# A decode kernel of two layers: the mixer's two halves of w3 in two PSUM banks, and a new order at the start of layer 2

## The chip, the cores and the metric

The kernel runs on one core of one Trainium2 chip. The metric is the time of one execution in microseconds (us), taken on the device. Before the change it was 529.77 us (median of 6 runs, 528.97 to 530.6). Every run also has a *span*, the time from the core's first to its last profiled instruction.

## The reference

One token (a row of 640) passes attention, mixer, attention, mixer; both layers use the same weights and caches.

```python
def _A_ref(x, k_cache, v_cache, wq, wo):          # 32 heads of 192
    W = 4096                                       # the last 4096 of 32768 positions
    q = (x @ wq) ...                               # one query for each head
    scores = einsum(q, k_cache[:, :, Sk - W:]) * 192 ** -0.5
    o = einsum(softmax(scores), v_cache[:, :, Sk - W:])
    return o @ wo
def _B_ref(x, w1, w2, w3, w4):
    ...                                            # with one token, the shifted part adds nothing
    h2 = gelu(layernorm(x1) @ w3) @ w4             # 640 -> 1536 -> 640
    return x1 + h2
x = x + _A_ref(layernorm(x), ...)                  # layer 1
x = x + _B_ref(layernorm(x), ...)
x = x + _A_ref(layernorm(x), ...)                  # layer 2, the same caches
x = x + _B_ref(layernorm(x), ...)
```

K and V of a head are 4096 x 192 bf16, 1536 KB each. Loading them is nearly all of the work.

## The kernel before

SBUF holds eleven *cells* of 1536 KB: one holds K or V of a head, transposed K, a block of wo, w3 or w4. A load is issued by the Sync engine's queue (SPq) in a fixed order, and each waits until its cell has been given back.

Layer 1 ends with heads 0 to 3, and layer 2 starts with them, to use again what is still on chip. K of heads 0 to 6 stays, transposed, in seven cells (the *kept* heads). V 3 stays in its cell. A part of V 2 stays in PSUM: while layer 1 uses V 2, VectorE turns (transposes) 22 units of 96 words per partition into four banks of PSUM and, for what doesn't fit there, into the free end of the bank in which O is accumulated. At the start of layer 2 it turns them back into SBUF. Only the rest of V 2 is loaded again.

In the views PE is TensorE, PEld its loading of weights, DVE VectorE and ACT ScalarE. *PV* is the product of a head's softmax weights (`PT`) with its V, which TensorE accumulates in the bank of O. K 8 is K of head 8, V 2 is V of head 2.

```python
VC, VP, VW = 3, 2, 22 * Dh // 2        # kept V, parked V, parked words per partition
...
O_bank = psO.tile([P, 512], F32, name="O_ps")      # one bank
O_ps = O_bank[:, 0:2 * Dh]
VB = 2048
V_bank = psV.tile([P, VB], F32, name="V_ps")       # four banks
VX = 2 * Dh, 2 * Dh + VW - VB

def v_words(layer):                    # layer 0: SBUF -> PSUM; layer 1: PSUM -> SBUF
    V = need("v", layer, VP)
    step = 512
    for i in range(0, VW, step):
        n = min(step, VW - i)
        a = V[:, 2 * i:2 * (i + n)].bitcast(U32)
        b = (V_bank[:, i:i + n] if i < VB else O_bank[:, VX[0]:VX[1]]).bitcast(U32)
        nc.vector.transpose(b if layer == 0 else a, a if layer == 0 else b)
```

(In the code layers are 0 and 1; the text says layer 1 and layer 2.) The first step of attention in layer 2, with the next heads 4 to 7 of which 4, 5 and 6 are kept:

```python
# after the scores of heads 0..3
q1[0]()            # PE: the projection of heads 4..7, 30 matmuls
q1[1]()
part_max()         # DVE: softmax of heads 0..3 begins
q1[2]()
turn_max()
q1[3]()
full_max()
for i, (q2, h2) in enumerate(keep):          # scores of heads 4, 5, 6
    for half in range(2):
        T(h2, half)
        S(h2, half, ST_n, q2)
    if i == 0:
        spread_max()
turn_p()
need("v", 1, cur[-1] + 1)
q[0]()
PT = swap()
...
q[2]()
v_words(1)         # the turn of V 2, just ahead of the first PV
q[3]()
```

The mixer's first product, in both layers. One column of `hp` holds 128 of the 1536 outputs and takes five matmuls:

```python
for half in range(2):
    hp = O_bank[:, VX[1] + half * HF:VX[1] + (half + 1) * HF]    # both in the bank of O
    for i in range(HF):                                          # HF = 6
        for kc in range(ND):                                     # ND = 5
            nc.tensor.matmul(hp[:, i:i + 1], lhsT=w3[kc][:, ...], rhs=xc[:, kc:kc + 1], ...)
    h_ps.append(hp)
for half, hp in enumerate(h_ps):
    nc.scalar.activation(sq[:], hp, ACTF.Square, scale=rr[:, 0:1])
    ...                                                          # the rest of gelu, then hT
# then 60 matmuls of w4, of which the first 30 need half 0 alone
```

Of the kernel before, what the change touches and what calls it, by code (L numbers as in the profile page):

```python
# [9 lines left out]
F32 = mybir.dt.float32  # L10
U32 = mybir.dt.uint32
# [6 lines left out]
P = 128  # L18
# [8 lines left out]
def kernel(  # L27
# [16 lines left out]
    _, H, Sk, Dh = A_k_cache.shape  # L44
# [6 lines left out]
    ND, NF = D // P, F // P  # L51
# [12 lines left out]
    NA = Dh // 32  # L64
    NKEEP, NCELL = 7, 11
    WARM = 29
    VC, VP, VW = 3, 2, 22 * Dh // 2
    W3C, W4C = FREE // F, FREE // D
    assert W4C % 2 == 1 and W4C < NF
    GROUPS = [[list(range(h, h + QH)) for h in range(0, H, QH)] for _ in range(2)]  # L70
# [9 lines left out]
    psV = ctx.enter_context(tc.tile_pool(name="psV", bufs=1, space=PSUM))  # L80
# [4 lines left out]
        name=nc.get_next_instruction_name(), act_func_set_id=ACT_TABLE_SET, ins=[], outs=[]))  # L85
# [381 lines left out]
    O_bank = psO.tile([P, 512], F32, name="O_ps")  # L467
    nc.vector.memset(O_bank[:], 0.0)
    O_ps = O_bank[:, 0:2 * Dh]
    VB = 2048  # L470
    V_bank = psV.tile([P, VB], F32, name="V_ps")
    VX = 2 * Dh, 2 * Dh + VW - VB

    def v_words(layer):
        V = need("v", layer, VP)
        step = 512
        for i in range(0, VW, step):
            n = min(step, VW - i)
            a = V[:, 2 * i:2 * (i + n)].bitcast(U32)
            b = (V_bank[:, i:i + n] if i < VB else O_bank[:, VX[0]:VX[1]]).bitcast(U32)  # L480
            nc.vector.transpose(b if layer == 0 else a, a if layer == 0 else b)

    def pv(layer, h, hq, PT, mid=None):
# [41 lines left out]
    def attention(layer, x_cur, rs_cur, x_new, z_new, rs_new, ss_new):  # L525
# [8 lines left out]
        def softmax_scale():  # L534
            rstd = power(total()[:, 0:1], 1.0 / D, eps1[:], "rstd")
            nc.vector.tensor_scalar(out=sc[:], in0=rstd[:], scalar1=scale, scalar2=None, op0=ALU.mult)
# [51 lines left out]
        q1 = qproj_steps(groups[1][0] // QH, xc)  # L588
        for hq, h in enumerate(groups[0]):
            for half in range(2):  # L590
                if layer == 0:
                    T(h, half)
                else:
                    Th.update({(h, q): transpose_quart(layer, h, q) for q in (2 * half, 2 * half + 1)})
                S(h, half, ST, hq)
                if (hq, half) == (0, layer):
                    qb[2]()
                    qb[3]()
            if hq == 1:
                softmax_scale()  # L600
        pending = None
        early = None
        for gi, cur in enumerate(groups):
            nxt = list(enumerate(groups[gi + 1])) if gi + 1 < len(groups) else []
            ST_n = None
            if nxt:
                part_max, turn_max, full_max, spread_max, turn_p, swap, recip = softmax_steps(len(cur), ST, sc)
                ST_n = next_scores()
                if layer == 1 and gi == 0:
                    keep = [hh for hh in nxt if hh[1] < NKEEP]  # L610
                    del nxt[:len(keep)]
                    q = qproj_steps(groups[2][0] // QH, xc)
                    q1[0]()
                    q1[1]()
                    part_max()
                    q1[2]()
                    turn_max()
                    q1[3]()
                    full_max()
                    for i, (q2, h2) in enumerate(keep):  # L620
                        for half in range(2):
                            T(h2, half)
                            S(h2, half, ST_n, q2)
                        if i == 0:
                            spread_max()
                    turn_p()
                    need("v", 1, cur[-1] + 1)
                    q[0]()
                    PT = swap()
                    q[1]()  # L630
                    rl = recip()
                    q[2]()
                    v_words(1)
                    q[3]()
                else:
                    if gi == 0:
                        for step in q1:
                            step()
                    h0 = nxt[0][1]
                    T(h0, 0)  # L640
                    part_max()
                    T(h0, 1)
                    S(h0, 0, ST_n, 0)
                    turn_max()
                    full_max()
                    S(h0, 1, ST_n, 0)
                    spread_max()
                    h1 = nxt[1][1]
                    q = None
                    if gi + 2 < len(groups):  # L650
                        q = qproj_steps(groups[gi + 2][0] // QH, xc)
                    if q:
                        q[0]()
                    if pending is not None:
                        y_ps = out_proj(layer, *pending)
                    turn_p()
                    T(h1, 0)
                    if q:
                        q[1]()
                        q[2]()  # L660
                    if pending is not None:
                        add_y(y_ps, 2)
                        pending = None
                    PT = swap()
                    T(h1, 1)
                    if q:
                        q[3]()
                    rl = recip()
                    nxt.pop(0)
            else:  # L670
                PT, rl = early
            oT = sm.tile([P, NA], BF16, name="oT")
            hurry = gi + 2 == len(groups)
            final = gi + 1 == len(groups)
            fold = None
            order = list(enumerate(cur))
            if layer == 1 and gi == 0:
                order.insert(0, order.pop(cur.index(VC)))
            for hq, h in order:
                o_sb = pv(layer, h, hq, PT, fold)  # L680
                if final:
                    if layer == 0 and hq == 0:
                        add_y(out_proj(layer, *pending), 1)
                    if layer == 0 and hq == 1:
                        center_y()
                    fold = None
                    if hq < QH - 2:
                        o_fold(h, o_sb, oT, rl)
                    else:
                        def fold(h=h, o_sb=o_sb):  # L690
                            o_fold(h, o_sb, oT, rl)

                    continue
                if hurry and hq == 1:
                    (q2, h2), (q3, h3) = nxt
# [3 lines that stand above are left out]
                    T(h3, 0)  # L699
                    S(h3, 0, ST_n, q3)  # L700
                    T(h3, 1)
                elif hurry and hq == 2:
                    S(h3, 1, ST_n, q3)
                    steps = softmax_steps(len(cur), ST_n, sc)
                    steps[0]()
                    steps[1]()
                elif nxt and not (hurry and hq == 3):
                    q2, h2 = nxt.pop(0)
# [3 lines that stand above are left out]
                o_fold(h, o_sb, oT, rl)  # L712
                if hurry and hq == 2:
                    steps[2]()
                if hurry and hq == 3:
                    for step in steps[3:5]:
                        step()
                    early = steps[5](), steps[6]()
            if final:
                if layer == 1:  # L720
                    y_ps = out_proj(layer, *pending)
                    fold()
                    add_y(y_ps, 1)
                    center_y()
                else:
                    fold()
            pending = (cur[0] // QH, oT)
            ST = ST_n
        add_y(out_proj(layer, *pending), 0)

    def mixer(layer, x_cur, z, rs_cur, ss_cur, x_new, rs_new):
# [23 lines left out]

        HF = NF // 2
        hT = big.tile([P, NF], BF16, name="hT")
        h_ps = []
        for half in range(2):
            hp = O_bank[:, VX[1] + half * HF:VX[1] + (half + 1) * HF]  # L760
            for i in range(HF):
                fc = half * HF + i
                f0 = 2 * P * (fc // 2) + fc % 2
                for kc in range(ND):
                    nc.tensor.matmul(
                        hp[:, i:i + 1], lhsT=w3[kc][:, f0:f0 + 2 * P - 1:2], rhs=xc[:, kc:kc + 1],
                        start=(kc == 0), stop=(kc == ND - 1))
            h_ps.append(hp)
        for half, hp in enumerate(h_ps):
            sq = sm.tile([P, HF], F32, name="sq")  # L770
            nc.scalar.activation(sq[:], hp, ACTF.Square, scale=rr[:, 0:1])
# [75 lines left out]
```

## Time and profile before

| what | before | where to read it |
|---|---|---|
| time | 529.77 us, 6 runs | times |
| moved by DMA | 217.31 MB, 98.0% of 16 engines' span | page |
| rate, 20 to 285 us and 305 to 500 us | 423 to 430 GB/s | windows |
| rate, 285 to 305 us (between the layers) | 345 GB/s | windows |
| busy: PE, DVE | 60%, 54% | page |
| last wo landed, then serial work to the end | 516.85 us, about 12 us (to the end of the span, 528.6 us) | chain of waits |

These are lines of the page of the kernel before: the span, TensorE's busy time, what the DMA engines moved, the main queue, and the share of each engine in the chain of waits that ended last.

```profile
span 528.6 us, 10089 instructions
PE 318.6 (60%) x4421; PEld 194.2 (37%) x4421; DVE 285.1 (54%) x557; ACT 41.0 (8%) x157; POOL 2.7 (1%) x12
...
DMA packets 23823, 217.31 MB, mean 411 GB/s; under 512 B 2532, under 2 KB 3044, under 8 KB 8292
...
q1 hardware_dynamic: 23780, 216.67, 98.0%
...
DMA 47%; PE 27%; DVE 20%; issue 4%; ACT 1%; SPq 1%; DVEq 0%; ACTq 0%
```

The next view gives the windows of the kernel before. The columns are the stretch, its length, busy time of each engine with the number of instructions, and at the end the granted clock, the DMA engines' busy share and GB/s.

```profile
20.00:285.00 265.00, 160.06 (x2042) 94.82 (x2043) 150.08 (x257) 17.37 (x66) 0.00 (x0) 0.67 1.01 423
285.00:305.00 20.00, 16.00 (x401) 12.85 (x399) 5.92 (x38) 3.78 (x17) 0.00 (x0) 0.68 0.90 345
305.00:320.00 15.00, 8.62 (x125) 4.64 (x121) 8.30 (x17) 0.78 (x3) 0.00 (x0) 0.66 1.02 430
```

The DMA engines are full (a share of 1.01 or 1.02) before and after the stretch between the layers, and not in it. A chain of waits with PE and DVE in it does not contradict this: each load waits for a cell, but while several loads are queued nothing is lost by that wait. Time can only be won where the DMA engines run dry, from 285 to 305 us, and in the tail, after the last load that anything waits for.

The timeline of the kernel before, in the first mixer. Columns: start, duration, engine, line, operation, out<-in, number, and in brackets the idle time ahead and what ended it.

```profile
286.93 0.24 PE L765 MATMUL O_ps<-xc,cell_2816 128*128 128x1 bf16 x4
...
288.50 0.17 PE L765 MATMUL O_ps<-xc,wx_sb 128*128 128x1 bf16 x1
...
288.76 0.27 ACT L771 ACTIVATE sq<-O_ps,r 128x6 f32<-128x6 f32 x1 [0.85 <-PE O_ps L765]
...
289.46 0.25 ACT L771 ACTIVATE sq<-O_ps,r 128x6 f32<-128x6 f32 x1
...
290.13 1.11 PE L792 MATMUL y_ps<-hT,cell_2995 128*128 128x1 bf16 x33 [1.47 <-DVE gu L773]
```

The 60 matmuls of w3 run from 286.93 to 288.67 us. The first Square reads only half 0, which was complete after 30 of them, but it starts at 288.76, after all 60, released by PE.

The same view at the start of layer 2: the turn of V 2 in five pieces (4 + 1), and the first PV matmuls.

```profile
306.66 2.49 DVE L481 STREAM_TRANSPOSE cell_3350<-V_ps 128x512 uint32<-128x512 uint32 x4
309.07 0.21 DVE L481 STREAM_TRANSPOSE cell_3350<-O_ps 128x64 uint32<-128x64 uint32 x1
...
309.33 1.45 PE L492 MATMUL O_ps<-cell_2819,PT 128*2 128x384 bf16 x16 [2.72 <-DVE cell_3350 L481]
```

And the Sync queue's timeline: when loads went out.

```profile
285.82 0.33 SPq L127 DMA_DIRECT2D cell_3344<-in_A_v_cache_dram  x1
291.92 0.33 SPq L127 DMA_DIRECT2D cell_3346<-in_A_v_cache_dram  x1
295.85 0.33 SPq L109 DMA_DIRECT2D cell_3348<-in_A_k_cache_dram  x1
...
299.45 0.33 SPq L109 DMA_DIRECT2D cell_3354<-in_A_k_cache_dram  x1
```

The load at 291.92 goes into the cell that w4 leaves at the end of the first mixer; the one at 295.85 into the cell of the first kept head, after its scores.

### The profile page before, as it was taken

The numbers are of one execution on the slowest core, as the hardware profiler recorded it, in microseconds if no ns is written. First come the engines' busy times: TensorE is split into PE (matmuls) and PEld (weight loads), VectorE is DVE, ScalarE is ACT, GpSimd is POOL, SyncE is SP. The second block draws the span as 40 slices with busy tenths as digits, with TensorE's granted clock in tenths as the row PEclk, the third lists the DMA queues.
The fourth block names the chain that finished last, engine by engine and source line by source line (L and its number), as shares of the span: only waits on it lengthen the run. The fifth ranks groups of instructions, "written<-read, shape, count | busy, mean of one in ns | idle before, by whom it ended". The sixth has DMA issues, their size and how long they took to land.

```text
span 528.6 us, 10089 instructions
## 1 busy us (share of the span) xinstructions
PE 318.6 (60%) x4421; PEld 194.2 (37%) x4421; DVE 285.1 (54%) x557; ACT 41.0 (8%) x157; POOL 2.7 (1%) x12
## 2 busy tenths in 40 slices
PE   1057657666563755746654865666666655647755
PEld 1023434343341533424323633434343433424325
DVE  2067655576464665556632255666665664646623
ACT  1000101010100001001101101010010001001011
POOL 2000000000000000000000000000000000000000
PEclk9999975557666576557655767675567676557655
DMA  8999999999999999999999899999999999999993
GB/s 346 430 423 425 423 427 425 422 426 421 427 424 421 425 424 426 423 425 423 424 408 391 326 428 428 421 425 421 428 422 427 424 424 425 423 425 422 425 411 127
DMA packets 23823, 217.31 MB, mean 411 GB/s; under 512 B 2532, under 2 KB 3044, under 8 KB 8292
## 3 DMA queue, kind: packets, MB, share of 16 engines
q1 hardware_dynamic: 23780, 216.67, 98.0%
q8 instruction: 34, 0.56, 0.4%
q14 instruction: 9, 0.07, 0.0%
HBM read 216.66 MB, written 0.00 MB: 410 GB/s over the span
## 4 chain that ended last, share of the span: by engine, by line
DMA 47%; PE 27%; DVE 20%; issue 4%; ACT 1%; SPq 1%; DVEq 0%; ACTq 0%
PE ST_ps L384 11%; DVE cell_240 L330 8%; PE O_ps L492 7%; DVE cell_3443 L330 7%; DMA cell_1696<-in_A_k_cache_dram 5%; DMA cell_2027<-in_A_k_cache_dram 5%; DMA cell_5426<-in_A_v_cache_dram 5%; DMA cell_1365<-in_A_k_cache_dram 5%; DMA cell_4862<-in_A_k_cache_dram 5%; DMA cell_238<-in_A_k_cache_dram 4%; DMA cell_4531<-in_A_k_cache_dram 4%; DMA cell_5624<-in_A_wo_dram 4%; DMA cell_2361<-in_A_k_cache_dram 4%; DMA cell_2819<-in_A_v_cache_dram 3%; DMA cell_2598<-in_A_v_cache_dram 2%
## 5 line engine op out<-in xcount | busy, mean ns | idle before, releaser
L384 PEld LDWEIGHTS <-Qblk 128*16 128x16 bf16 x1536 | 87.1, 112 | 191.9 <-issue 166.2
L500 DVE STREAM_TRANSPOSE o_sb<-O_ps 128x384 f32<-128x384 f32 x64 | 37.3, 583 | 125.8 <-PE O_ps L492 125.8
L384 PE MATMUL ST_ps<-cell_240,Qblk 128*16 128x256 bf16 x600 | 70.3, 391 | 54.2 <-DVE cell_240 L330 39.3
L384 PE MATMUL ST_ps<-cell_3443,Qblk 128*16 128x256 bf16 x600 | 69.6, 391 | 48.5 <-DVE cell_3443 L330 32.0
L492 PEld LDWEIGHTS <-PT 128*2 128x2 bf16 x1024 | 45.0, 103 | 31.9 <-issue 19.4
L508 ACT ACTIVATE oT<-oT_ps,rl 32x6 bf16<-32x6 f32 x64 | 16.5, 258 | 292.0 <-PE oT_ps L507 285.4
L507 PEld LDWEIGHTS oT_ps<-o_sb,Lq 128*32 128x32 f32 x256 | 21.7, 147 | 27.4 <-issue 22.0
L507 PE MATMUL oT_ps<-o_sb,Lq 128*32 128x6 f32 x256 | 22.5, 197 | 14.7 <-DVE o_sb L500 14.4
L437 DVE STREAM_TRANSPOSE PrT<-Pr 128x256 bf16<-128x256 bf16 x16 | 7.1, 445 | 33.8 <-PE qT_ps L346 23.0
L346 PE MATMUL qT_ps<-xc,wq_sb 128*128 128x1 bf16 x480 | 15.8, 165 | 13.5 <-DMA wq_sb<-in_A_wq_dram 12.7
L346 PEld LDWEIGHTS <-wq_sb 128*128 128x128 bf16 x480 | 14.6, 103 | 15.1 <-DMA wq_sb<-in_A_wq_dram 13.7
L360 PE MATMUL Qrep_ps<-Xq,Lb 128*128 128x24 bf16 (+1 forms) x18 | 3.3, 182 | 21.5 <-DVE Xq L353 21.4
L353 DVE TENSOR_TENSOR Xq<-qT_ps,maskq 128x24 bf16<-128x24 f32 (+1 forms) x18 | 2.8, 156 | 20.5 <-PE qT_ps L346 20.5
L448 PEld LDWEIGHTS <-Eq 128*32 128x32 bf16 x256 | 4.7, 113 | 24.2 <-issue 24.1
L453 PE MATMUL l_ps<-lh,ones 128*128 128x4 f32 x32 | 8.8, 346 | 5.3 <-ACT PT L451 5.3
L453 PEld LDWEIGHTS l_ps<-lh,ones 128*128 128x128 f32 x32 | 7.4, 288 | 8.0 <-ACT PT L451 7.6
L429 ACT COPY nb_sb<-nb_ps 128x1 f32<-128x1 f32 x16 | 2.6, 160 | 98.0 <-PE nb_ps L426 97.8
L448 PE MATMUL PT_ps<-PrT,Eq 128*32 128x32 bf16 x256 | 7.2, 236 | 4.1 <-DVE PrT L437 4.1
L432 ACT ACTIVATE Pr<-ST_ps,nb_sb,sc 128x256 bf16<-128x256 f32 x16 | 9.0, 565 | 0.5
L426 PEld LDWEIGHTS nb_ps<-ones,PrT 1*128 1x128 f32 x32 | 6.8, 262 | 5.7 <-issue 5.7
L426 PE MATMUL nb_ps<-ones,PrT 1*128 1x1 f32 x32 | 8.1, 321 | 0.0
L451 ACT CAST PT<-PT_ps 128x128 bf16<-128x128 f32 x16 | 4.3, 266 | 43.2 <-PE PT_ps L448 43.2
(285 smaller groups left out, 472.3 us busy)
## 6 DMA issues: line engine op xcount, KB each, us to landing
wq_sb<-in_A_wq_dram SPq DMA_DIRECT2D x5, 1536.0 KB, 12.8
cell_238<-in_A_k_cache_dram SPq DMA_DIRECT2D x1, 1536.0 KB
cell_272<-in_A_k_cache_dram SPq DMA_DIRECT2D x1, 1536.0 KB, 25.1
cell_309<-in_A_k_cache_dram SPq DMA_DIRECT2D x1, 1536.0 KB, 25.8
cell_339<-in_A_k_cache_dram SPq DMA_DIRECT2D x1, 1536.0 KB
cell_405<-in_A_k_cache_dram SPq DMA_DIRECT2D x1, 1536.0 KB, 30.7
cell_484<-in_A_v_cache_dram SPq DMA_DIRECT2D x1, 1536.0 KB, 30.7
cell_486<-in_A_k_cache_dram SPq DMA_DIRECT2D x1, 1536.0 KB, 30.7
```

Of the source, the lines that this page charges most:

```text
L330: nc.vector.transpose(Tu, Ku[:, :, q * NY:(q + 1) * NY])
L346: nc.tensor.matmul(qT_ps[:, tl:tl + 1], lhsT=wq_sb[:, kc, t * P:(t + 1) * P], rhs=xc[:, kc:kc + 1], start=(kc == 0), stop=(kc == ND - 1))
L384: nc.tensor.matmul(ST_ps[r:r + QW, :].rearrange("p (g i) -> p g i", g=ng), lhsT=Q[:, n, :], rhs=T4[:, :, f, :, t], start=(hq == 0 and n == ...
L426: nc.tensor.matmul(nb_ps[:], lhsT=held["w"], rhs=ones[0:1, 0:1], start=True, stop=True)
L432: nc.scalar.activation(out=Pr[:], in_=ST_ps, func=ACTF.Exp, bias=nb_sb[:, 0:1], scale=sc[:, 0:1], accum_out=lpart[:, 0:1])
L437: nc.vector.transpose(held["PrT"][:], held["Pr"][:])
L448: nc.tensor.matmul(PT_ps[32 * m:32 * (m + 1), :, :, ng * q:ng * (q + 1)], lhsT=Eq[:, q, :], rhs=src[:, m:QW:NM], start=True, stop=True)
L453: nc.tensor.matmul(l_ps[:], lhsT=ones[:], rhs=held["lh"][:], start=True, stop=True)
L492: nc.tensor.matmul(O_ps[r:r + 2, :], lhsT=PT[:, hq, 2 * i:2 * i + 2], rhs=V[:, 2 * i * Dh:2 * (i + 1) * Dh], start=(i < 4), stop=(i >= NB ...
L500: nc.vector.transpose(o_sb[:], O_ps.rearrange("p (e a c) -> p e c a", e=2, c=NA))
L507: nc.tensor.matmul(oT_ps[r, :], lhsT=Lq[:], rhs=o_sb[:, e, :, e], start=(e == 0), stop=(e == 1))
L508: nc.scalar.activation(oT[r, :], oT_ps[r, :], ACTF.Copy, scale=rl[r, 0:1])
```

## The change

The intent was twofold. With the two halves of w3 in two PSUM banks, gelu of half 0 can run beside the matmuls of half 1. In layer 2, all kept heads are scored ahead of the first softmax, so that their cells come free earlier, and V 2 is turned back beside these scores instead of right in front of the first PV. To make room, one unit less of V 2 is kept (21 in place of 22), and no part of it in the bank of O.

```diff
-    VC, VP, VW = 3, 2, 22 * Dh // 2
+    VC, VP, VW = 3, 2, 21 * Dh // 2
...
-    VB = 2048
-    V_bank = psV.tile([P, VB], F32, name="V_ps")
-    VX = 2 * Dh, 2 * Dh + VW - VB
+    V_bank = psV.tile([P, 2048], F32, name="V_ps")
+    h_ps = V_bank[:, VW:VW + NF // 2], O_bank[:, 2 * Dh:2 * Dh + NF // 2]
...
-            b = (V_bank[:, i:i + n] if i < VB else O_bank[:, VX[0]:VX[1]]).bitcast(U32)
+            b = V_bank[:, i:i + n].bitcast(U32)
...
             if hq == 1:
                 softmax_scale()
+            if hq == 2 and layer == 1:
+                q1[0]()
+                q1[1]()
...
-                    q1[0]()
-                    q1[1]()
-                    part_max()
                     q1[2]()
-                    turn_max()
                     q1[3]()
-                    full_max()
-                    for i, (q2, h2) in enumerate(keep):
+                    v_words(1)
+                    for q2, h2 in keep:
                         for half in range(2):
                             T(h2, half)
                             S(h2, half, ST_n, q2)
-                        if i == 0:
-                            spread_max()
-                    turn_p()
+                    for step in (part_max, turn_max, full_max, spread_max, turn_p):
+                        step()
...
                     q[2]()
-                    v_words(1)
                     q[3]()
...
-        h_ps = []
-        for half in range(2):
-            hp = O_bank[:, VX[1] + half * HF:VX[1] + (half + 1) * HF]
+        for half, hp in enumerate(h_ps):
...
-            h_ps.append(hp)
```

## The prediction

> **What bounds it now.** The DMA engines. The page gives 217.31 MB, the main queue busy 98.0% of 16 engines' span; the windows view shows 424 to 426 GB/s in nearly every stretch of 20-285 us and 305-500 us. PE is busy 60%, DVE 54%. The chain of waits is 47% DMA; its PE and DVE pieces lie where the queue is full anyway. So time can be won only where the DMA engines run dry: (a) between the layers, 285-305 us: 345 GB/s at a busy share of 0.90, dry for about 2.5 us in all (20 us x (1.02 - 0.90)), most at 285-288, 291-294 and 297-300; (b) the tail after the last wo lands at 516.8 us, 11 us of serial work.
>
> **Mixer (both layers).** Timeline: the 60 matmuls of w3 take 1.74 us (286.93 to 288.67), and ScalarE's first Square waits for all 60, though it needs 30 (released by PE, starts 288.76). The Trainium skill, "PSUM — Partial Sum Buffer", section "PSUM bank collisions raise a hardware error", says that a dependency is added between any two instructions on different engines that touch the same bank and quadrant; this trace agrees. With two banks the Square can start after 30 matmuls, about 287.95 (the scale r is ready at 287.91). Gelu half one, then the w4 matmuls (before: 290.13), move about 0.8 us earlier; half two follows 0.9 us later, as before, just in time after 30 matmuls of w4.
> - Layer 2's mixer is pure tail: -0.8 us. Its w4 has landed by 522.7, needed at 523.1.
> - Layer 1's: its end releases the load issued at 291.92 and then those at 295.85 to 299.45. Issued 0.8 us earlier, they shorten the dry stretch 291-294: -0.5 to -0.8 us (w4's last part lands at 290.1, just when wanted).
>
> **Layer 2's start.** Moved: the projection (0.90 us) ahead of the fourth head's scores, all three kept heads (0.7 us each) ahead of the softmax, V 2's turn (2.55 us, 306.66 to 309.28, on which the first PV at 309.33 waits) now in their shadow. PV starts 2.5 to 3 us earlier beyond the mixer's gain, and loads issued at 302.0 and 304.9 go out 1 to 2 us earlier. But the queue already holds work there: issue to landing takes 13 to 15 us, and 305-320 us moves 430 GB/s. So worth 0 to 0.2 us: the compute lead becomes longer waits for K later.
>
> **V 2's share.** 96 words per partition less are kept in PSUM: 128 x 192 x 2 B = 49 KB more to load, at 424 GB/s +0.12 us, fully on the path. In layer 1 PV 2 no longer waits 3.17 us for the turn into its bank; the next V lands at 282.86 by DMA, so 0.
>
> **Sum.** -0.8 -0.7 -0.1 +0.1 = -1.5: **528.2 us**, 527.3 to 529.1. Chances: faster by over 2% 0.01, within 2% 0.98, slower 0.01.
>
> **In the profile.** Right if: Square starts 0.9 us after the first w3 matmul (now 1.8); w4's matmuls start 0.8 us sooner in both mixers; first PV of layer 2 waits for PT and starts near 306; dry time at 285-305 falls by about 0.7 us, later rate unchanged; waits for K in layer 2 grow.
>
> **Wrong if:** the Square still waits for all 60; w4 or the next cell gates the refill; the DMA rate in layer 2 profits from the earlier releases; or the extra load shifts the end.

## The result, and the profile after

The changed kernel took 528.46 us (median of 10 runs, 527.95 to 529.32) against 529.95 us (20 runs). The ratio is 0.9971, with a 95% interval of 0.9963 to 0.998: 0.3% faster, clear of noise, and far within 2%. A ratio is the mean time of one kernel's runs over that of the other's runs of the same rounds, so it is not quite the ratio of the medians.

The page of the changed kernel:

```profile
span 526.8 us, 10085 instructions
PE 323.5 (61%) x4421; PEld 196.5 (37%) x4421; DVE 284.8 (54%) x555; ACT 41.1 (8%) x157; POOL 2.7 (1%) x12
...
DMA packets 23823, 217.35 MB, mean 413 GB/s; under 512 B 2532, under 2 KB 3044, under 8 KB 8420
...
q1 hardware_dynamic: 23780, 216.72, 98.4%
...
DMA 50%; PE 24%; DVE 20%; issue 4%; ACT 1%; SPq 1%; DVEq 0%
```

The windows of the changed kernel:

```profile
20.00:285.00 265.00, 160.36 (x2051) 95.14 (x2051) 149.99 (x256) 17.36 (x66) 0.00 (x0) 0.65 1.01 423
285.00:305.00 20.00, 17.10 (x379) 12.61 (x376) 7.57 (x39) 3.02 (x14) 0.00 (x0) 0.56 0.95 365
305.00:320.00 15.00, 9.47 (x151) 5.62 (x151) 7.08 (x17) 1.85 (x7) 0.00 (x0) 0.77 1.01 430
```

From 20 to 285 us and from 305 to 320 us the rate is the same. Between the layers, 365 GB/s against 345 over 20 us are 0.4 MB more moved, worth 0.94 us at 424 GB/s in this pair of profiles (the pair is at the upper end; see the experiments).

The timeline of the changed kernel, first mixer:

```profile
286.69 0.24 PE L759 MATMUL V_ps<-xc,cell_2815 128*128 128x1 bf16 x4
...
287.73 0.27 ACT L764 ACTIVATE sq<-V_ps,r 128x6 f32<-128x6 f32 x1
...
288.26 0.17 PE L759 MATMUL O_ps<-xc,wx_sb 128*128 128x1 bf16 x1
...
288.47 0.27 ACT L764 ACTIVATE sq<-O_ps,r 128x6 f32<-128x6 f32 x1
...
289.10 1.11 PE L785 MATMUL y_ps<-hT,cell_2994 128*128 128x1 bf16 x33 [0.67 <-DVE gu L766]
```

The first Square now starts 1.04 us after the first matmul (before: 288.76 - 286.93 = 1.83 us) and ahead of the last w3 matmul of half 1 at 288.26 us. The matmuls of w4 start 2.41 us after it (before: 3.20 us). Both moved by 0.79 us. In both kernels the w4 matmuls were released by VectorE (the bracket), not by the load of w4. The Square no longer waits for PE at all: the timeline has ScalarE finish the layernorm's scale r at 287.68 us, when the last matmul of half 0 ends as well (287.63 us). So r is the next bound here, and a further split of w3 alone could not move the first Square. This agrees with what the Trainium skill states in "PSUM — Partial Sum Buffer", section "PSUM bank collisions raise a hardware error": guard PSUM by bank and quadrant, not by address. Half 0's reader had waited for writes to other columns of its bank.

The second mixer, which is in the tail, before:

```profile
522.51 0.27 ACT L771 ACTIVATE sq<-O_ps,r 128x6 f32<-128x6 f32 x1 [0.85 <-PE O_ps L765]
...
523.88 1.11 PE L792 MATMUL y_ps<-hT,cell_5815 128*128 128x1 bf16 x33 [1.47 <-DVE gu L773]
```

and after:

```profile
520.75 0.27 ACT L764 ACTIVATE sq<-V_ps,r 128x6 f32<-128x6 f32 x1
...
522.12 1.11 PE L785 MATMUL y_ps<-hT,cell_5813 128*128 128x1 bf16 x33 [0.67 <-DVE gu L766]
```

From the Square to the first w4 matmul it is 1.37 us in both kernels. The w4 matmuls start 1.76 us earlier; 0.96 us of that was there when the mixer's input was ready (518.61 against 519.57 us in the timelines), and 0.80 us was won in the mixer itself.

The Sync queue's timeline of the changed kernel, with the loads that were shown of before:

```profile
285.59 0.33 SPq L127 DMA_DIRECT2D cell_3253<-in_A_v_cache_dram  x1
290.88 0.33 SPq L127 DMA_DIRECT2D cell_3255<-in_A_v_cache_dram  x1
294.81 0.33 SPq L109 DMA_DIRECT2D cell_3257<-in_A_k_cache_dram  x1
...
300.51 0.33 SPq L109 DMA_DIRECT2D cell_3357<-in_A_k_cache_dram  x1
```

The loads released by the mixer went out 1.04 us earlier in this pair (of which 0.23 us was there before the mixer began: 285.59 against 285.82). The load of K 8 went out 1.06 us *later*, because the projection now comes ahead of the fourth head's scores.

The start of layer 2 in the changed kernel: the turn in four pieces, the softmax's first step, and the first PV.

```profile
300.81 2.47 DVE L480 STREAM_TRANSPOSE cell_3259<-V_ps 128x512 uint32<-128x512 uint32 x4
...
303.98 0.42 DVE L404 TENSOR_REDUCE pm<-ST_ps 128x1 f32<-128x256 f32 x1 [0.70 <-PE ST_ps L384]
...
308.39 0.82 PE L491 MATMUL O_ps<-cell_2818,PT 128*2 128x384 bf16 x16
```

Here the prediction missed. The turn lies beside the scores, and PV does not wait for it; yet PV starts at 308.39 us, 0.94 us earlier than before, not near 306 us. It is no earlier than the mixer's gain alone would have made it.

### The profile page after: what moved, and what is told of

Read it like the earlier page. It is cut to its first block, busy times and chain, and to the rows that moved or that the text cites. A ratio compares the mean times of both kernels' runs of the same rounds, so it can differ in the third digit from the quotient of the medians.

```text
span 526.8 us, 10085 instructions
## 1 busy us (share of the span) xinstructions
PE 323.5 (61%) x4421; PEld 196.5 (37%) x4421; DVE 284.8 (54%) x555; ACT 41.1 (8%) x157; POOL 2.7 (1%) x12
## 4 chain that ended last, share of the span: by engine, by line
DMA 50%; PE 24%; DVE 20%; issue 4%; ACT 1%; SPq 1%; DVEq 0%
PE ST_ps L384 10%; DVE cell_3441 L330 8%; PE O_ps L491 6%; DVE cell_240 L330 6%; DMA cell_1696<-in_A_k_cache_dram 6%; DMA cell_1365<-in_A_k_cache_dram 5%; DMA cell_2027<-in_A_k_cache_dram 5%; DMA cell_5424<-in_A_v_cache_dram 5%; DMA cell_1034<-in_A_k_cache_dram 5%; DMA cell_4860<-in_A_k_cache_dram 5%; DMA cell_5622<-in_A_wo_dram 4%; DMA cell_238<-in_A_k_cache_dram 4%; DMA cell_2361<-in_A_k_cache_dram 4%; DMA cell_2818<-in_A_v_cache_dram 3%; DMA cell_2575<-in_A_k_cache_dram 2%
## 5 line engine op out<-in xcount | busy, mean ns | idle before, releaser
L384 PE MATMUL ST_ps<-cell_240,Qblk 128*16 128x256 bf16 x600 | 69.5, 386 | 54.0 <-DVE cell_240 L330 39.1
L384 PE MATMUL ST_ps<-cell_3441,Qblk 128*16 128x256 bf16 x600 | 70.5, 393 | 46.6 <-DVE cell_3441 L330 31.2
L491 PEld LDWEIGHTS <-PT 128*2 128x2 bf16 x1024 | 46.4, 105 | 30.7 <-issue 14.3
L384 PE MATMUL ST_ps<-cell_2363,Qblk 128*16 128x256 bf16 x48 | 4.4, 410 | 4.9 <-DVE pm L404 4.6
```

What stands on the lines that cost most here:

```text
L384: nc.tensor.matmul(ST_ps[r:r + QW, :].rearrange("p (g i) -> p g i", g=ng), lhsT=Q[:, n, :], rhs=T4[:, :, f, :, t], start=(hq == 0 and n == ...
L491: nc.tensor.matmul(O_ps[r:r + 2, :], lhsT=PT[:, hq, 2 * i:2 * i + 2], rhs=V[:, 2 * i * Dh:2 * (i + 1) * Dh], start=(i < 4), stop=(i >= NB ...
```

## The experiments

Twelve kernels were run, five rounds each, in three sets of four, each set on one chip together with the kernel before. Spans are means of the runs; "against before" is the difference from the mean of the kernel before in the same set.

| run | what it is | ratio to before (95%) | span | span against before |
|---|---|---|---|---|
| base21 | before, 21 units of V 2, none in the bank of O | 1.0013 (1.0 to 1.0025) | 528.12 | +0.39 |
| banks_only | base21 + two banks | 0.998 (0.9966 to 0.9993) | 526.64 | -1.09 |
| order_only | base21 + new order | 1.0008 (0.9995 to 1.002) | 528.14 | +0.41 |
| after_again | base21 + both = the changed kernel | 0.9977 (0.9964 to 0.9989) | 526.50 | -1.23 |
| first_only | changed, two banks in the first mixer only | 0.9994 (0.9981 to 1.0008) | 527.48 | -0.26 |
| second_only | changed, two banks in the second mixer only | 0.9993 (0.9978 to 1.0008) | 527.40 | -0.35 |
| late_turns | changed, V 2 turned twice more ahead of PV | 0.9982 (0.9967 to 0.9997) | 526.82 | -0.93 |
| keep9 | changed, 9 units of V 2 kept | 1.0013 (0.9998 to 1.0028) | 528.40 | +0.65 |
| q1_later | changed, projection behind the fourth head | 0.9973 (0.996 to 0.9986) | 526.58 | -1.40 |
| v22 | changed, 22 units kept, still two banks | 0.9971 (0.9959 to 0.9984) | 526.54 | -1.44 |
| banks22 | v22 in the old order | 0.9974 (0.996 to 0.9987) | 526.76 | -1.22 |
| best22 | v22 + q1_later | 0.997 (0.9958 to 0.9983) | 526.46 | -1.52 |

The standard error of such a mean of spans is 0.04 to 0.26 us, and that of a difference of two of them 0.2 to 0.4 us, so differences below about 0.4 to 0.7 us are not told apart from nothing. All twelve gave correct results.

### The change taken apart: base21, banks_only, order_only, after_again

Theory: the DMA engines set the pace, so the two banks are the whole gain (one mixer refills the dry stretch, the other is in the tail) and the new order gives nothing. Rival: part of the gain comes from the order, whose PE and DVE work is in the chain of waits.

base21 is the changed kernel with the old order and both halves in the bank of O:

```diff
-    h_ps = V_bank[:, VW:VW + NF // 2], O_bank[:, 2 * Dh:2 * Dh + NF // 2]
+    h_ps = O_bank[:, 2 * Dh:2 * Dh + NF // 2], O_bank[:, 2 * Dh + NF // 2:2 * Dh + NF]
...                                              # and the order of q1, softmax, keep and v_words as before
```

> The kernel before with one change alone: 96 words per partition less of V 2 kept in PSUM (so 49 KB more loaded, and no V words in the bank of O). One bank for both halves of w3, old order of layer 2. Theory (DMA engines bound; bytes count, DVE turns in layer 1 do not): +0.12 us against the kernel before, 530.0 to 530.2 us. Rival (the turn of V 2 that PV 2 of layer 1 waits for, 3.2 us, is on the path): 1 to 3 us faster than before.

> base21 plus the two PSUM banks in the mixer, old order of layer 2. Theory: the banks are the whole gain, 0.8 us in the tail and 0.7 us in the dry stretch between the layers: 1.5 us below base21, the time of the changed kernel (528.4) within 0.3 us. Rival (the new order of layer 2 gives half of the gain): 0.8 us below base21 at most.

> base21 plus the new order of layer 2, both halves of w3 in one bank. Theory: PV of layer 2 starts earlier, but the DMA engines set the pace: within 0.3 us of base21. It might even lose some tenths, as the load of K 8 goes out 1 us later (300.51 against 299.45 in the two traces) because the projection was put ahead of the fourth head. Rival: 0.7 to 1 us below base21.

> The changed kernel as it is, in the rounds of the others, so that they can be compared on one chip: 528.4 us, ratio 0.997. In the profile the granted clock at 298 to 303 us, which was 0.5 in the changed kernel and 1.0 in the one before, may differ again: if it does from run to run, the late first PV (308.39 us) is put down to the clock and not to the order.

Edits of the other three: banks_only takes back only the change of order, order_only only the change of `h_ps`, after_again nothing.

Measured, in mean spans: the banks give 526.64 - 528.12 = -1.48 us in the old order and 526.50 - 528.14 = -1.64 us in the new one. The order gives 528.14 - 528.12 = +0.02 us with one bank and 526.50 - 526.64 = -0.14 us with two, both within the noise. So the banks are the gain, and the order is worth nothing that these runs can show. base21's own +0.39 us (times: +0.66 us) is above the 0.12 us expected, but its interval reaches down to nothing. One of its five runs took 3.2 us beyond its span where others took 1.7 to 2.1, which is why its times look worse than its spans. The rival for base21, that the turn which PV 2 of layer 1 waits for is on the path, fell: that wait (3.17 us in the kernel before) is gone, and base21 is not faster.

base21 also shows what the first PV of layer 2 had waited for. Its timeline, with the turn still in its old place:

```profile
305.96 0.33 PE L491 MATMUL O_ps<-cell,PT 128*2 128x384 bf16 x3
306.08 2.46 DVE L480 STREAM_TRANSPOSE cell<-V_ps 128x512 uint32<-128x512 uint32 x4
```

The first PV of order_only and of after_again, in the new order:

```profile
307.51 0.82 PE L491 MATMUL O_ps<-cell,PT 128*2 128x384 bf16 x16
```

```profile
306.89 1.45 PE L491 MATMUL O_ps<-cell,PT 128*2 128x384 bf16 x16
```

In base21 PV starts at 305.96 us and the turn runs beside it. Not the place of the turn but its last piece, in the bank of O, had held PV back: O's matmuls write that bank. The changed order is in fact later: order_only's first PV starts at 307.51 us and after_again's at 306.89 us, while base21's and banks_only's start at 305.96 and 305.58 us. In the new order the softmax begins only when the scores of all three kept heads are done, and its steps follow one another with nothing beside them.

after_again settled the granted clock too. These are windows of 298 to 300 us; the third number from the end is the granted clock. First the kernel before, then the changed kernel's first profile, then after_again, which is the same code.

```profile
298.00:300.00 2.00, 2.00 (x75) 1.65 (x68) 0.15 (x1) 0.34 (x2) 0.00 (x0) 1.00 0.81 301
```

```profile
298.00:300.00 2.00, 2.00 (x54) 1.57 (x54) 0.18 (x1) 0.00 (x0) 0.00 (x0) 0.50 0.91 338
```

```profile
298.00:300.00 2.00, 1.65 (x59) 1.26 (x56) 0.51 (x3) 0.00 (x0) 0.00 (x0) 1.00 0.96 362
```

The same kernel was granted 0.50 in one execution and 1.00 in another. The Trainium skill, "TensorE: Matmul & The Clock Gate", section "What's actually happening", says that the clock gate judges activity in a free-running window, so that the transition differs from run to run. It does differ here, but by more than the 500 ns either way that the section gives: the clock rose at about 302.5 us in the first profile and at about 297.6 us in after_again. With the full clock the first PV of the changed kernel starts at 306.89 us, with half of it at 308.39 us. The time does not follow it visibly: v22's profile had 0.50 from 298 to 302 us and a span of 527.0 us, q1_later's had 1.00 and 527.1 us.

### Each mixer alone: first_only, second_only

```diff
-        for half, hp in enumerate(h_ps):
+        for half, hp in enumerate(h_of[layer]):   # h_of: two banks in one layer, the bank of O in the other
```

> The changed kernel with two banks in layer 1's mixer alone; layer 2's has both halves in one bank. Theory: the tail gets its wait back, +0.8 us against the changed kernel, 529.2 us; the trace shows the dry stretch as in the changed kernel and ScalarE's first Square of the second mixer 1.83 us after its first matmul.

> The changed kernel with two banks in layer 2's mixer alone. Theory: the loads after 291 us go out 0.8 us later again and the dry stretch grows by as much: +0.7 us, 529.1 us. Rival (the DMA queue has work enough between the layers, the first mixer does not count): as the changed kernel, 528.4 us.

Measured against the kernel before in the same rounds, spans are -0.26 us (first_only) and -0.35 us (second_only), where the changed kernel in its set had -1.23 us. So the second mixer's banks are worth 0.97 us and the first one's 0.88 us, with standard errors of 0.3 and 0.4 us: each near the 0.8 and 0.7 us expected, together 1.85 us where the direct comparison gave 1.5 to 1.6 us. Counted from the other side, from order_only, which has one bank in both mixers (+0.41 us), first_only gains 0.67 us and second_only 0.75 us, together 1.42 us. All of these comparisons cross two sets. The rival, that the first mixer does not count, is contradicted by 0.88 us, a little over two standard errors, and by the dry stretch below.

The timelines show the mechanism returning where it was put back. first_only, second mixer:

```profile
521.48 0.27 ACT L766 ACTIVATE sq<-O_ps,r 128x6 f32<-128x6 f32 x1 [0.85 <-PE O_ps L761]
```

second_only, first mixer:

```profile
288.45 0.27 ACT L766 ACTIVATE sq<-O_ps,r 128x6 f32<-128x6 f32 x1 [0.85 <-PE O_ps L761]
```

In both the Square waits 0.85 us for PE again, as in the kernel before. The dry stretch follows the first mixer alone. From 285 to 305 us the four profiles with one bank in the first mixer (before, base21, order_only, second_only) moved 345, 352, 340 and 339 GB/s, 344 on average; the ten with two banks there moved 352 to 365, 356.5 on average (the groups touch at 352). Over 20 us the difference is 0.25 MB, or 0.59 us at 424 GB/s. The pair of profiles first looked at had shown 0.94 us: single profiles scatter here.

### More work on VectorE at the start of layer 2: late_turns

```diff
                     q[2]()
+                    v_words(1)
+                    v_words(1)
                     q[3]()
```

> The changed kernel with the turn of V 2 done three times: once where it is, twice more just ahead of the first PV's evictions (the same data again; the result stays right). DVE gets 4.9 us of work more at about 308 us. Theory (DMA-bound after 305 us, the queue 13 us deep): 0 to 0.3 us slower. Rival (the chain of PE and DVE from 309 to 410 us, which the profile shows as the chain that ended last, sets the time): 2.5 to 5 us slower.

```profile
307.00 4.82 DVE L480 STREAM_TRANSPOSE cell<-V_ps 128x512 uint32<-128x512 uint32 x8
...
307.04 1.45 PE L491 MATMUL O_ps<-cell,PT 128*2 128x384 bf16 x16
...
311.88 0.56 DVE L499 STREAM_TRANSPOSE o_sb<-O_ps 128x384 f32<-128x384 f32 x1
```

The first PV ran at 307.04 us, but its result was turned out of PSUM only at 311.88 us, after 4.82 us of added transposes. The span was 0.93 us below the kernel before, 0.3 us short of the changed kernel's 1.23 us, and the difference is within the noise. Nearly all of 4.8 us disappeared. Where it went can be read at the DMA queue. The next three loads of wo were issued at 326.42, 355.72 and 384.38 us here and at 322.88, 352.17 and 380.77 us in after_again, some 3.5 us later each. But the DMA engines moved 430 GB/s from 305 to 320 us and 423 GB/s from 320 to 400 us (after_again: 429 and 424), for the loads only stood in the queue for less time. These are the loads of K from 305 to 400 us, with the median from issue to landing in us at the end, first of late_turns and then of after_again:

```profile
cell<-in_A_k_cache_dram SPq DMA_DIRECT2D x13, 1536.0 KB, 18.3
```

```profile
cell<-in_A_k_cache_dram SPq DMA_DIRECT2D x13, 1536.0 KB, 21.2
```

The chain of waits ran through PE and DVE in this stretch, and still 4.8 us of DVE work in it cost next to nothing. This agrees with the new order gaining nothing.

### More to load: keep9

```diff
-    VC, VP, VW = 3, 2, 21 * Dh // 2
+    VC, VP, VW = 3, 2, 9 * Dh // 2
```

> The changed kernel with 12 units of 96 words less of V 2 kept in PSUM: 590 KB more to load (12 x 49,152 B), but only 43% of the words to turn. Theory: 590 KB at 424 GB/s, +1.39 us, 529.8 us, so 0.116 us for one unit. Rival (the turn of V 2 counts): 0 or faster.

The span rose from 1.23 us below the kernel before to 0.65 us above it: +1.9 us for 590 KB, 0.16 us for a unit. The sign and the size are the theory's, and the rival (fewer words to turn, so faster) fell. The 1.9 us have a standard error of 0.34 us, so they are not told apart from the 1.39 us of a rate of 424 GB/s. By 305 us keep9's one profile had moved no more than the others (352 GB/s in the stretch between the layers), although its larger load of V 2 was issued inside that stretch, so there is no sign that it filled the dry time.

### The order within the new order, and the 22nd unit: q1_later, v22, banks22, best22

q1_later moves the projection back behind the fourth head:

```diff
-            if hq == 2 and layer == 1:
-                q1[0]()
-                q1[1]()
...
+                    q1[0]()
+                    q1[1]()
                     q1[2]()
```

v22 puts the 22nd unit back, into the bank of O, and the second half of w3 behind it:

```diff
+    VB = 21 * Dh // 2
+    VO = 2 * Dh + VW - VB                        # VW is 22 units again
-    h_ps = V_bank[:, VW:VW + NF // 2], O_bank[:, 2 * Dh:2 * Dh + NF // 2]
+    h_ps = V_bank[:, VB:VB + NF // 2], O_bank[:, VO:VO + NF // 2]
```

banks22 is v22 in the old order, best22 is v22 with q1_later's edit.

> The changed kernel with the projection for the next heads moved back behind the fourth head's scores (the three kept heads are still all scored ahead of the softmax). K 8's load, which the fourth head's area is freed for, should go out some 0.9 us earlier, the next two loads about 0.5 us later. Theory (at 300 us three loads are already queued, so these issue times do not count): span within 0.3 us of the changed kernel's 526.5 us, 1.2 us below the kernel before. Rival (the late K 8 load costs what the new order gains): 0.5 us or more below the changed kernel.

> The changed kernel with the 22nd unit of V 2 kept in PSUM again: 96 words in the bank of O, and the second half of w3 behind them in the same bank, so the two halves still have two banks. 49 KB less to load. Theory: 0.12 us (49 KB at 424 GB/s) to 0.16 us (a twelfth of what keep9's 12 units cost in spans) below the changed kernel, 1.35 to 1.4 us below the kernel before; too little to be told apart from nothing in one set of rounds. Rival (base21's 0.4 to 0.7 us is what one unit costs): 0.5 us or more below the changed kernel.

> As v22 but with the old order of layer 2, so it is the kernel before with nothing changed except where the mixer's two halves lie. Theory (the banks are the whole gain): as v22, 1.4 us below the kernel before; the first PV of layer 2 waits for the turn again (which touches the bank of O), near 308 us, without cost. Rival (the late first PV, or the order, counts): 0.5 us or more slower than v22.

> v22 and q1_later together: the candidate for the fastest. Theory: within 0.3 us of v22, 1.4 us below the kernel before.

Spans against before were -1.40, -1.44, -1.22 and -1.52 us: all within 0.3 us of each other and of the changed kernel. The load of K 8 went out at 298.23 us in q1_later and at 299.56 us in after_again, and the time did not show it. The 22nd unit's 0.12 to 0.16 us is too small for these runs. banks22 is the cleanest statement of the result: nothing but where the halves of w3 lie differs from the kernel before, and it has the gain. Its timeline also confirms what base21 showed: with a part of V 2 in the bank of O, PV waits for the turn again, here 2.72 us.

```profile
307.77 0.24 DVE L482 STREAM_TRANSPOSE cell<-O_ps 128x96 uint32<-128x96 uint32 x1
308.07 1.45 PE L493 MATMUL O_ps<-cell,PT 128*2 128x384 bf16 x16 [2.72 <-DVE cell L482]
```

That wait cost nothing that can be measured (span 526.76 us against v22's 526.54 us, whose PV did not wait). best22 was the candidate for the fastest and has the smallest span of all twelve, but it is not told apart from the changed kernel.

## Why the prediction was right or wrong

The predicted time, 528.2 us, lies 0.26 us below the measured 528.46 us, within the range, and the predicted gain of 1.5 us is the measured one (529.95 - 528.46 = 1.49 us). The interval of the ratio leaves 1.1 to 2.0 us for the gain, so that it agrees to the hundredth is chance; that the two mixers carry it is not. One step failed, the start of PV in layer 2, and it did not count. Point by point:

- **"Time can be won only where the DMA engines run dry": right, as far as it was tested.** late_turns added 4.8 us of DVE work to the chain outside these places, and the span rose by 0.3 us, within noise. First_only and second_only changed things inside these places and moved the span by 0.7 to 1.0 us each.
- **"The Square can start after 30 matmuls ... the w4 matmuls move about 0.8 us earlier": right.** 0.79 us in the first mixer. The Square starts 1.04 us after the first w3 matmul, not 0.9, as r is ready only then. The wait of 0.85 us comes back to the hundredth where one bank is put back.
- **"Layer 2's mixer is pure tail: -0.8 us": right** (first_only: 0.97 us by difference of spans, standard error 0.3 us; 0.80 us within the mixer in the timelines).
- **"Layer 1's: ... -0.5 to -0.8 us": right** (second_only: 0.88 us, standard error 0.4 us; bytes moved from 285 to 305 us: 0.59 us).
- **"PV starts 2.5 to 3 us earlier beyond the mixer's gain", "now in their shadow": wrong in the size and in the cause.** In the first profile it was 0.94 us earlier in all. With the full clock granted, as in the kernel before, it started at 306.89 us (after_again): 2.4 us earlier in all, of which 0.8 us are the mixer's and 0.4 us were there before the mixer began (285.42 against 285.82 us), so some 1.2 us in place of 2.5 to 3. The estimate used matmul times taken at the full clock and left out that the softmax's steps now stand in line after the scores. And not the shadow freed PV: base21 left the turn in its old place and PV started at 305.96 us, because no piece of V 2 was in the bank of O any more. The diff had been read as two changes of order; it was the same matter of banks a second time.
- **"Loads issued at 302.0 and 304.9 go out 1 to 2 us earlier": it depends on the granted clock.** In the first profile, at half clock, they went out at 302.45 and 303.97 us, one 0.4 us later and one 0.9 us earlier. In after_again, at the clock of the kernel before, they went out at 300.89 and 302.25 us, 1.1 and 2.6 us earlier (the mixer's 0.8 us and the 0.4 us from before it included). K 8's load, which the prediction did not look at, went out 1.06 and 0.11 us later.
- **"So worth 0 to 0.2 us": right.** The order gave -0.14 to +0.02 us. The error in the step before did no harm, since the step does not count for the time.
- **"Waits for K in layer 2 grow": not shown.** From 309 to 516 us VectorE's waits for K sum to 9.0 us in the profile of before and 6.5 us in that of the changed kernel, but they also range from 6.5 to 8.9 us between two profiles of the changed kernel. late_turns, at the full clock, has 6.6 us. What sets these sums was not found.
- **"V 2's share ... +0.12 us": not contradicted, and too small to be measured alone.** keep9 gives 0.16 us for a unit (standard error 0.03 us), base21 0.39 us with an interval down to nothing.

## What to carry to other kernels

In this kernel two engines that use one PSUM bank wait for each other even where they touch different columns, so look for readers that wait for the last of a group of writes when they need only the first; giving the parts two banks overlaps them, here at no cost that banks22 shows. Before counting a wait as time, find the places where the bounding resource runs dry and ask whether the wait ends there: here 0.8 us in such a place was worth 0.7 to 1.0 us, and 4.8 us elsewhere next to nothing. When one change holds several parts, run each part alone, for the part with the most lines in the diff may carry none of the gain.

## What the Trainium skill lacked or had wrong

- "PSUM — Partial Sum Buffer", section "PSUM bank collisions raise a hardware error": the rule is there and agrees with the traces that were read, but not its price nor how to see it in a profile. Here it was 0.85 us of ScalarE waiting for matmuls of other columns, and 2.72 to 3.17 us of PE waiting for VectorE's transposes of data parked at the end of its bank.
- "TensorE: Matmul & The Clock Gate", section "What's actually happening": it has the clock rise after one window of about 3.4 us of sustained work. In the changed kernel's first profile PE was busy in every half microsecond from 293.5 to 300.5 us, longer than two such windows, and still was granted 0.50 until about 302.5 us; in after_again the clock rose at about 297.6 us with the same instructions. How busy a window must be is not stated.
- "DMA: Bandwidth & Descriptors", section "Bandwidth": nothing wrong was found. Its 425 GB/s for large transfers, taken with loads issued from GpSimd, agrees with the 423 to 425 GB/s of the long stretches here, with loads issued by the Sync engine.
